# Gated attention and two MLP blocks on Trainium2: the input statistics taken as one maximum on VectorE, the gate's statistics on row sums of the output

## The chip, the core and the metric

The kernel runs on one core of a Trainium2 chip. The core has five engines with queues of their own, each working in order: TensorE (PE in the profile; its weight loads are PEld), VectorE (DVE), ScalarE (ACT), GpSimd (POOL) and SyncE (SP), which here issues all DMAs. They meet at semaphores: an instruction that reads what another engine or a DMA writes waits for it, and so does one that overwrites what another still reads. The metric is device time in microseconds; before the change its median is 695.99 us over three runs (694.93 to 697.37).

## The reference

Inputs q, k, v, alpha have 4 batches, 8 heads, 768 positions and head width 48. A gated linear attention is followed by a ReLU block and a gated block, both with residuals, all in float32:

```python
state = zeros(B, H, D, D)
for t in range(S):
    state = alpha[:, :, t, :, None] * state + einsum('bhd,bhe->bhde', k[:, :, t], v[:, :, t])
    y[:, :, t] = einsum('bhd,bhde->bhe', q[:, :, t], state)
x = y.transpose(0, 2, 1, 3).reshape(B, S, 384)
x = x + maximum(layer_norm(x) * g1 @ w1, 0) @ w2              # 384 -> 1536 -> 384
u, v = split(gelu_tanh(x @ w_in), 2)                          # 384 -> 1024
v = layer_norm(v) * g2
x = x + (u * (w_sg @ v + b_sg)) @ w_out                       # w_sg is 768 x 768 over positions
```

## The kernel before

The positions of a batch are cut into six chunks of 128 rows, so there are 24 chunks, and two neighbouring chunks form a group for the ReLU block. `split_path` computes everything with float32 numbers split into a high and a low float16 half, three matmul passes for each product. This is exact enough only while numbers stay in certain bounds, so it gathers statistics as it goes (`st_in` of the inputs, `st_fe` of the decay, `st_xs` and `st_xm` of the residual stream, `st_g` of the gate, `st_ws` of the weights). At its end a list `checks` compares them with bounds (three small DVE instructions for each entry, L1039 to L1041), the results are reduced to one flag `bad`, and only if it is set does `general_path` compute all of it again without splitting.

The work comes in steps and units. A chunk's attention is a list of steps (`att_steps`); the dense blocks are units: A (L675, matmuls into `pg`, then the two halves of `hT`, L680 on ACT and L681 on DVE), B (L709, L712), T (L730, transposes), C (L749, L774), D (the gate over positions: matmuls L794, `tm` on DVE L800, product on POOL L803, halves on ACT L804 and POOL L805, and a square with a sum on ACT, L807) and E (output matmuls L822, the residual added by DVE L824, the store L826). Steps and units have due times from a table of numbers, and Python emits them in that order; a scheduler of the tile framework then reorders instructions within each engine by a simulated timeline. What stands in an engine's queue is therefore read from the built program.

`load_chunk` (L236) loads alpha, q, k and v of a chunk into one of two buffers `inp`, so chunk i + 2 overwrites chunk i, operand by operand, as soon as the last reader of that operand is done. Readers are: for alpha, q and k the copies to `stage` on ACT (L295), whose tiles SP transposes by DMA (L298) and ACT copies once more (L311) before the decay scans on DVE (L351, L354); for v the split into two halves `vs` (L151 on ACT, L152 on DVE); and `stats` for all four. `stats` takes three squares with row sums on ACT (L532, for q, k and v) and one maximum of magnitudes on DVE (L534, for alpha). The first batch's six chunks, called whole, take no statistics, so `stats` runs for 18 chunks. The load of chunk i + 2 stands in the emitted order behind the `stats` of chunk i.

Of the kernel before, what the change touches and what calls it, by code (L numbers as in the profile page):

```python
# [7 lines left out]
F32 = mybir.dt.float32  # L8
# [4 lines left out]
AF = mybir.ActivationFunctionType  # L13
ALU = mybir.AluOpType
AX = mybir.AxisListType
PSUM = bass.MemoryType.PSUM

P = 128
# [35 lines left out]
def split_path(ctx, tc, ident, bad, q, k, v, alpha, g1, w1, w2, w_in, g2, w_sg, b_sg, w_out, out):  # L54


    nc = tc.nc
    B, H, S, D = q.shape
    DM = H * D
    NP = H // 2  # L60
    NCH = S // P
# [6 lines left out]
    NC = B * NCH  # L68
# [8 lines left out]
    big = ctx.enter_context(tc.tile_pool(name="big", bufs=1))  # L77
# [19 lines left out]
    st_in = big.tile([P, NC, 4], F32, name="st_in")  # L97
# [1 line left out]
    st_mv = big.tile([P, NC, 2], F32, name="st_mv")  # L99
    st_xs = big.tile([P, NC], F32, name="st_xs")  # L100
    st_xm = big.tile([P, NC], F32, name="st_xm")
    st_g = big.tile([P, NC], F32, name="st_g")
    st_ws = big.tile([P, 8 + NG3 + 2 * KD], F32, name="st_ws")
    st_w, st_wg, st_w1, st_wr = (st_ws[:, a:b] for a, b in ((0, 8), (8, 8 + NG3), (8 + NG3, 8 + NG3 + KD),
                                                            (8 + NG3 + KD, 8 + NG3 + 2 * KD)))
# [5 lines left out]
    def junk():  # L111
        return p2.tile([P, 512], BF16, tag="cv", name="junk")
# [141 lines left out]
    def att_steps(i, group, slot):  # L254
        b, c = divmod(i, NCH)
        t = inp[i % NIN]
# [133 lines left out]
        if i >= KA:  # L390
            n = NP * (P + 1)
# [124 lines left out]
        if whole:  # L516
            T["vs"] = t[:, 2, :, 0:D]
        else:
            @step
            def _():  # L520
                T["vs"] = p1.tile([P, 2, H, D], F16, tag="vs", name="vs")
                split2(T["vs"][:, 0], T["vs"][:, 1], t[:, 2, :, 0:D], S_V)

            stats_step[i] = len(steps)

            @step
            def _():
                stats()

        def stats():  # L530
            for n in range(3):
                nc.scalar.activation(out=junk()[:, 0:DM].rearrange("p (h d) -> p h d", h=H), in_=t[:, n, :, 0:D],  # L532
                                     func=AF.Square, accum_out=st_in[:, i, n:n + 1])
            nc.vector.tensor_reduce(out=st_in[:, i, 3:4], in_=t[:, 3, :, 0:D], op=ALU.max, axis=AX.XY,  # L534
                                    apply_absolute_value=True)

        @step
        def _():
# [120 lines left out]
    def A_units(j):  # L659


        units = []
        N, per = (P, KD) if j == 0 else (U, 512 // U)
        for part in range(U // N):
            for u in range(KF // per):
                def unit(u=u, part=part):
                    m = part if j == 0 else u // (KF // per // 2)
                    if (j, m) not in hT:
                        hT[j, m] = ring.tile([P, 2, KF * P], F16, tag="hT", bufs=2, name="hT")
                    pg = ps.tile([P, per, N], F32, tag="g", bufs=3, name="pg")  # L670
                    o = slice(part * N, (part + 1) * N)
                    for f in range(per):
                        ff = u * per + f
                        for n_, (kk, a, r) in enumerate([(kk, a, r) for kk in range(KD) for a, r in passes]):
                            nc.tensor.matmul(out=pg[:, f, :], lhsT=w1s[:, a, kk, ff * P:(ff + 1) * P],  # L675
                                             rhs=xhT[j][:, r, kk, o], start=(n_ == 0), stop=(n_ == 3 * KD - 1))
                    u0 = u if j == 0 else u % (KF // per // 2)
                    hi, lo = (hT[j, m][:, a, u0 * per * N:(u0 + 1) * per * N] for a in range(2))
                    src = pg.rearrange("p f t -> p (f t)")
                    nc.scalar.activation(out=hi, in_=src, func=AF.Relu)  # L680
                    last_dve[0] = nc.vector.scalar_tensor_tensor(out=lo, in0=src, scalar=0.0, in1=hi, op0=ALU.max,  # L681
                                                                 op1=ALU.subtract)
                units.append((unit, per * 9 * N / 2400.0, (2, 3, 5, 6)[((u + 1) * per - 1) // KD],
                              groups[j][0] * NCH + groups[j][1] + (part if j == 0 else 1)))
        return units
# [96 lines left out]
    def D_units(b):  # L782
        units = []
        for th in range(S // U):
            for dp in range(KG // 2):
                def unit(th=th, dp=dp):
                    key = (b, th)

                    gt[key] = uf[key].bitcast(F16).rearrange("p (g a f t) -> p g a f t", g=KG // 2, a=2, f=2)
                    pg = ps.tile([P, 2, U], F32, tag="g", bufs=3, name="pgs")  # L790
                    for f in range(2):
                        d = 2 * dp + f
                        for n_, (s, a, r) in enumerate([(s, a, r) for s in range(NCH) for a, r in passes]):
                            nc.tensor.matmul(out=pg[:, f, :], lhsT=vn[b * NCH + s][:, a, d * P:(d + 1) * P],  # L794
                                             rhs=wgs[th][:, r, s, :], start=(n_ == 0),
                                             stop=(n_ == 3 * NCH - 1))
                    tm = p2.tile([P, 2, U], F32, tag="tm", name="tm")
                    for f in range(2):
                        d = 2 * dp + f
                        nc.vector.scalar_tensor_tensor(out=tm[:, f, :], in0=pg[:, f, :], scalar=g2c[:, d:d + 1],  # L800
                                                       in1=bbc[:, th * U:(th + 1) * U], op0=ALU.mult, op1=ALU.add)
                    o = slice(2 * dp, 2 * dp + 2)
                    nc.gpsimd.tensor_tensor(out=tm, in0=tm, in1=uT[key][:, o, :], op=ALU.mult)  # L803
                    nc.scalar.activation(out=gt[key][:, dp, 0], in_=tm, func=AF.Copy)  # L804
                    nc.gpsimd.tensor_tensor(out=gt[key][:, dp, 1], in0=tm, in1=gt[key][:, dp, 0], op=ALU.subtract)  # L805
                    n_ = b * 6 + 2 * th + dp
                    nc.scalar.activation(out=junk()[:, 0:512].rearrange("p (a b) -> p a b", a=2), in_=tm,  # L807
                                         func=AF.Square, accum_out=st_g[:, n_:n_ + 1])
                units.append((unit, 36 * U / 2400.0, NW[3]))
        return units  # L810

    def E_units(b):
        units = []
        for c in range(NCH):
            def unit(c=c):
                i = b * NCH + c
                key = (b, c // 2)
                o = slice((c % 2) * P, (c % 2) * P + P)
                pg = ps.tile([P, DM], F32, tag="g", bufs=3, name="pgo")
                for d in range(KG):  # L820
                    for a, r in passes:
                        nc.tensor.matmul(out=pg, lhsT=gt[key][:, d // 2, a, d % 2, o], rhs=wos[:, r, d, :],  # L822
                                         start=(d == 0 and a == 0 and r == 0), stop=(d == KG - 1 and r == 1))
                nc.vector.scalar_tensor_tensor(out=xs[i], in0=pg, scalar=1.0 / (S_G * S_WO), in1=xs[i],  # L824
                                               op0=ALU.mult, op1=ALU.add)
                nc.sync.dma_start(out=out[b, c * P:(c + 1) * P, :], in_=xs[i])  # L826
            units.append((unit, 12 * DM / 2400.0, NW[4]))
        return units
# [30 lines left out]
    if True:  # L859
# [18 lines left out]
        for _ in range(2):  # L878
            t = ring.tile([P, KG * U], I32, tag="uT", bufs=3, name="bits")[:, 0:768]
# [13 lines left out]
        for kk in range(KD):  # L893
            nc.vector.tensor_scalar(out=diags[0][:, kk], in0=ident, scalar1=g1c[:, kk:kk + 1], scalar2=None,
                                    op0=ALU.mult)
# [40 lines left out]
        for j in range(NG + 1):  # L936
            starts.append(sum(x[1] for x in flat))
            seq = []
            if j < NG:
                a = A_units(j)  # L940
# [22 lines left out]
        def at(t):  # L963
            return D0 + min(t, DX) * DS + max(t - DX, 0.0)
# [9 lines left out]
        for j in range(NG):  # L974
            b, c, n = groups[j]
# [3 lines left out]
            for s in range(n):  # L979
                i = b * NCH + c + s  # L980
# [20 lines left out]
        for f, cost, need, *chunk in flat:  # L1001
            t = max([t, at(now)] + [emitted[i][-1] + 1e-3 for i in chunk])
# [6 lines left out]
        for _, kind, f, need in sorted(events, key=lambda x: x[:2]):  # L1009
# [8 lines left out]
        row_scale_window()  # L1018

        checks = [  # L1020
            (st_in[:, :, 0:3], 2.0 ** -2, 2.0 ** 12, [NC, 3]),
            (st_in[:, :, 3:4], 0.0, 1.0, [NC, 1]),
            (st_fe, 2.0 ** -100, 1.0, [NC, NP]),
            (st_xs, -1e30, 1e30, [NC]),
            (st_mv[:, :, 1:2], 2.0 ** -22 * S_Y ** 2, 2.0 ** 3 * S_Y ** 2, [NC, 1]),
            (st_xm, 2.0 ** -12, 2.0 ** 14, [NC]),
            (st_g, 0.0, 2.0 ** 31, [NC]),
            (st_w, 2.0 ** -2, 127.0, [8]),
            (st_wg, 2.0 ** -2, 6e4, [NG3]),
            (st_w1, 2.0 ** -2, 2000.0, [KD]),  # L1030
# [4 lines left out]
        for n, (src, lo, hi, shape) in enumerate(checks):  # L1035
# [6 lines left out]
                                    axis=AX.XY if len(shape) == 2 else AX.X)  # L1042
# [242 lines left out]
```

## Time and profile before

| | before |
|---|---|
| median of three runs | 695.99 us (694.93 to 697.37) |
| the profiled execution | 693.09 us, its span 691.3 us |
| mean granted TensorE clock | 0.982 |
| VectorE, 0 to 130 us | 113.70 us busy |
| TensorE, 0 to 130 us | 104.89 us busy, clock 0.95 |
| `L807` accumulator reads on ACT | 24 of 188 ns |
| squares of `x` on ACT, L732 (they stay) | 24 of 512 ns |

The profile was taken on one execution; the span runs from its first to its last instruction. A busy time is the time in which an engine had an instruction under way, an idle time is put down to what ended it. The rows that matter most stand beside the sentences that use them in the prediction.

### The profile page before, as it was taken

The page shows a single profiled execution, that of the slowest core. Times are in us where ns is not written, and L with a number is a line of the kernel's source. Part 1 is how long each engine was busy: PE and PEld are TensorE (multiplying, and loading weights), DVE is VectorE, ACT ScalarE, POOL GpSimd, SP SyncE. Part 2 cuts the span into 40 slices and gives each one's busy share as a digit, 9 for nine tenths or more (in the row PEclk, how much of TensorE's full clock was granted, in tenths as well). Part 3 has the DMA queues.
Part 4 walks back from the last instruction along what each step waited for, and adds up shares of the span by engine and source line. Part 5 has one row for each costly group of instructions (what it writes and reads, how often), then busy time and mean ns, then how long its engine had stood idle before and what let it go on. Part 6 is the DMA issues. An engine that isn't in the chain of part 4 may idle for free.

```text
span 691.3 us, 14364 instructions
## 1 busy us (share of the span) xinstructions
PE 639.3 (92%) x5622; PEld 485.9 (70%) x5622; DVE 445.4 (64%) x876; ACT 412.9 (60%) x787; POOL 242.7 (35%) x462
## 2 busy tenths in 40 slices
PE   5999579899999989999999988999999979999996
PEld 3787467677677876677777875676677867676783
DVE  7899868677744676557744678668666386333325
ACT  3765535667874589588765599767653764332230
POOL 2122011334423760433532860532405670302261
PEclk9999879999999998999999999999999999999999
DMA  9996797739482359366362169644251602200102
GB/s 227 279 233 193 206 236 157 133 64 131 68 120 43 51 101 164 99 119 108 70 109 46 39 109 206 123 70 73 50 81 29 103 17 64 29 13 12 35 2 73
DMA packets 228636, 70.63 MB, mean 102 GB/s; under 512 B 219472, under 2 KB 222544, under 8 KB 228560
## 3 DMA queue, kind: packets, MB, share of 16 engines
q1 hardware_dynamic: 228560, 69.63, 52.6%
q8 instruction: 46, 0.75, 0.5%
q14 instruction: 30, 0.25, 0.1%
HBM read 35.79 MB, written 4.72 MB: 59 GB/s over the span
## 4 chain that ended last, share of the span: by engine, by line
PE 43%; DVE 19%; ACT 13%; DMA 13%; POOL 5%; issue 3%; SPq 2%; ACTq 0%; DVEq 0%
PE pg L709 12%; PE pg L675 8%; PE pgo L822 6%; PE pgu L774 5%; DMA stage<-stage 5%; PE pgv L749 4%; PE pgs L794 3%; ACT stage L311 2%; DMA wgs<-wsp 2%; ACT stage L295 2%; DVE K L354 2%; ACT junk L532 2%; DVE F L354 2%; DMA inp<-in_q_dram 2%; DMA inp<-in_alpha_dram 2%
## 5 line engine op out<-in xcount | busy, mean ns | idle before, releaser
L675 PE MATMUL pg<-xhT,w1s 128*128 128x256 f16 (+1 forms) x1404 | 153.8, 269 | 8.0 <-DVE hT L681 7.4
L675 PEld LDWEIGHTS <-w1s 128*128 128x128 f16 x1404 | 130.1, 100 | 26.3 <-issue 8.2
L709 PE MATMUL pg<-w2s,hT 128*128 128x384 f16 x864 | 144.6, 326 | 0.3 <-DVE hT L681 0.3
L709 PEld LDWEIGHTS <-hT 128*128 128x128 f16 x864 | 83.7, 98 | 54.0 <-issue 0.5
L794 PE MATMUL pgs<-wgs,vn 128*128 128x256 f16 x864 | 96.0, 273 | 0.0
L794 PEld LDWEIGHTS <-vn 128*128 128x128 f16 x864 | 84.0, 98 | 10.4
L681 DVE SCALAR_TENSOR_TENSOR hT<-pg,hT 128x512 f16<-128x512 f32 (+1 forms) x74 | 49.5, 672 | 54.1 <-ACT hT L680 54.0
L311 ACT ACTIVATE stage<-stage 128x1024 uint16<-128x1024 uint16 x48 | 64.6, 1353 | 19.1 <-DMA stage<-stage 18.6
L295 ACT ACTIVATE stage<-inp 128x1024 uint16<-128x1024 uint16 x48 | 49.8, 1050 | 24.5 <-DVE K L354 12.6
L774 PE MATMUL pgu<-x2T,wis 128*128 128x256 f16 x432 | 50.1, 273 | 2.1 <-DVE hT L681 1.9
L822 PE MATMUL pgo<-wos,uT 128*128 128x384 f16 x288 | 48.6, 326 | 2.7 <-DVE hT L681 2.7
L680 ACT ACTIVATE hT<-pg 128x512 f16<-128x512 f32 (+1 forms) x74 | 42.1, 572 | 13.2 <-PE pg L675 13.1
L749 PE MATMUL pgv<-wis,x2T 128*128 128x512 f16 x216 | 49.4, 379 | 0.4 <-DVE x L824 0.3
L155 POOL TENSOR_TENSOR qs<-F,qs 128x512 f16<-128x512 f32 x18 | 20.5, 1138 | 80.2 <-ACT qs L422 80.1
L774 PEld LDWEIGHTS <-wis 128*128 128x128 f16 x432 | 41.6, 98 | 8.6 <-DVE hT L681 2.3
L155 POOL TENSOR_TENSOR kh<-K,kh 128x512 f16<-128x512 f32 x17 | 20.5, 1207 | 72.5 <-ACT kh L444 71.2
L822 PEld LDWEIGHTS <-uT 128*128 128x128 f16 x288 | 27.8, 98 | 21.1 <-issue 3.5
L800 DVE SCALAR_TENSOR_TENSOR tm<-pgs,g2c,bbc 128x256 f32<-128x256 f32 x48 | 20.9, 476 | 32.6 <-PE pgs L794 14.8
L803 POOL TENSOR_TENSOR tm<-tm,uT 128x512 f32<-128x512 f32 x24 | 33.3, 1387 | 15.5 <-DVE tm L800 15.5
L749 PEld LDWEIGHTS <-x2T 128*128 128x128 f16 x216 | 20.7, 98 | 22.6 <-issue 0.6
L804 ACT ACTIVATE uT<-tm 128x512 f16<-128x512 f32 x24 | 14.9, 622 | 34.2 <-POOL tm L803 34.2
L805 POOL TENSOR_TENSOR uT<-tm,uT 128x512 f16<-128x512 f32 x24 | 28.2, 1174 | 17.2 <-ACT uT L804 17.2
(175 smaller groups left out, 1094.2 us busy)
## 6 DMA issues: line engine op xcount, KB each, us to landing
stage<-in_moe_w_ch_dram SPq DMA_DIRECT2D x24, 384.0 KB, 5.0
inp<-in_alpha_dram SPq DMA_DIRECT2D x24, 192.0 KB, 3.4
inp<-in_q_dram SPq DMA_DIRECT2D x24, 192.0 KB, 3.6
inp<-in_k_dram SPq DMA_DIRECT2D x24, 192.0 KB, 4.0
inp<-in_v_dram SPq DMA_DIRECT2D x24, 192.0 KB, 4.0
out_dram<-x SPq DMA_DIRECT2D x24, 192.0 KB, 2.1
stage<-in_moe_w_in_dram SPq DMA_DIRECT2D x4, 768.0 KB, 4.6
stage<-in_moe_w_sg_dram SPq DMA_DIRECT2D x6, 384.0 KB, 3.7
```

Source lines behind the costliest of these rows:

```text
L155: (nc.vector if on_dve else nc.gpsimd).tensor_tensor(out=out, in0=in0, in1=in1, op=ALU.subtract)
L295: nc.scalar.activation(out=sp, in_=t[:, n].rearrange("p h d -> p (h d)").bitcast(U16) .rearrange("p (x w) -> p w x", w=2), func=AF.Copy)
L311: nc.scalar.activation(out=words[:, :, :, gap:], in_=tr, func=AF.Copy)
L675: nc.tensor.matmul(out=pg[:, f, :], lhsT=w1s[:, a, kk, ff * P:(ff + 1) * P], rhs=xhT[j][:, r, kk, o], start=(n_ == 0), stop=(n_ == 3 * KD ...
L680: nc.scalar.activation(out=hi, in_=src, func=AF.Relu)
L681: last_dve[0] = nc.vector.scalar_tensor_tensor(out=lo, in0=src, scalar=0.0, in1=hi, op0=ALU.max, op1=ALU.subtract)
L709: nc.tensor.matmul(out=box[s], lhsT=hidden(a, f, s), rhs=w2s[:, r, f, :], start=(f == 0 and a == 0 and r == 0), stop=(f == KF - 1 and r == 1))
L749: nc.tensor.matmul(out=pg, lhsT=x2T[j][:, a, kk, o], rhs=wis[:, r, kk, DG:DI], start=(n_ == 0), stop=(n_ == 3 * KD - 1))
L774: nc.tensor.matmul(out=pg[:, f, :], lhsT=wis[:, a, kk, ff * P:(ff + 1) * P], rhs=x2T[j][:, r, kk, 0:N], start=(n_ == 0), stop=(n_ == 3 * K ...
L794: nc.tensor.matmul(out=pg[:, f, :], lhsT=vn[b * NCH + s][:, a, d * P:(d + 1) * P], rhs=wgs[th][:, r, s, :], start=(n_ == 0), stop=(n_ == 3 ...
L803: nc.gpsimd.tensor_tensor(out=tm, in0=tm, in1=uT[key][:, o, :], op=ALU.mult)
L822: nc.tensor.matmul(out=pg, lhsT=gt[key][:, d // 2, a, d % 2, o], rhs=wos[:, r, d, :], start=(d == 0 and a == 0 and r == 0), stop=(d == KG ...
```

## The change

`stats` becomes one instruction on DVE: the largest magnitude of each row of q, k, v and alpha in one reduction of 128x1536 to 128x4. The bounds on q, k and v become bounds on a magnitude rather than on a sum of squares. The gate's square on ACT (L807) is kept for the last batch alone; for the other three batches the output's residual addition on DVE also leaves its row sum in a new tile `st_o`, which one more entry of `checks` compares with ±1e30.

```diff
-    st_g = big.tile([P, NC], F32, name="st_g")
+    st_g = big.tile([P, 6], F32, name="st_g")
+    st_o = big.tile([P, NC - NCH], F32, name="st_o")
...
         def stats():
-            for n in range(3):
-                nc.scalar.activation(out=junk()[:, 0:DM].rearrange("p (h d) -> p h d", h=H), in_=t[:, n, :, 0:D],
-                                     func=AF.Square, accum_out=st_in[:, i, n:n + 1])
-            nc.vector.tensor_reduce(out=st_in[:, i, 3:4], in_=t[:, 3, :, 0:D], op=ALU.max, axis=AX.XY,
-                                    apply_absolute_value=True)
+            nc.vector.tensor_reduce(out=st_in[:, i, :], in_=t[:, :, :, 0:D], op=ALU.max, axis=AX.XY, apply_absolute_value=True)
...
-                    n_ = b * 6 + 2 * th + dp
-                    nc.scalar.activation(out=junk()[:, 0:512].rearrange("p (a b) -> p a b", a=2), in_=tm,
-                                         func=AF.Square, accum_out=st_g[:, n_:n_ + 1])
+                    if b == B - 1:
+                        n_ = 2 * th + dp
+                        nc.scalar.activation(out=junk()[:, 0:512].rearrange("p (a b) -> p a b", a=2), in_=tm,
+                                             func=AF.Square, accum_out=st_g[:, n_:n_ + 1])
...
                 nc.vector.scalar_tensor_tensor(out=xs[i], in0=pg, scalar=1.0 / (S_G * S_WO), in1=xs[i],
-                                               op0=ALU.mult, op1=ALU.add)
+                                               op0=ALU.mult, op1=ALU.add,
+                                               accum_out=st_o[:, i:i + 1] if b < B - 1 else None)
...
-            (st_in[:, :, 0:3], 2.0 ** -2, 2.0 ** 12, [NC, 3]),
+            (st_in[:, :, 0:3], 2.0 ** -3, 3.25, [NC, 3]),
...
-            (st_g, 0.0, 2.0 ** 31, [NC]),
+            (st_g, 0.0, 2.0 ** 31, [6]),
+            (st_o, -1e30, 1e30, [NC - NCH]),
```

The lines move: the maximum is L532 in the changed kernel, and lines between there and L800 have a number smaller by three (hT's DVE half is L678, the `vs` and `xsp` splits are L153). Since every load now hangs on another instruction, the scheduler's order changes in more places than the diff touches.

The first place is DVE between chunks 11 and 13, near 246 to 257 us of the profile before. The two `inp` buffers are inp_94 and inp_95 before, inp_95 and inp_96 after, for even and odd chunks. Before:

```order
L155 TENSOR_TENSOR ss_3034<-sc,ss_3034 128x512
L800 SCALAR_TENSOR_TENSOR tm<-pgs,g2c,bbc 128x256 x2
L534 TENSOR_REDUCE st_in<-inp_94 128x1
L800 SCALAR_TENSOR_TENSOR tm<-pgs,g2c,bbc 128x256 x2
L609 TENSOR_TENSOR state<-psd,state 64x4x48 x2
L621 BN_STATS bs<-psy 128x6
L623 BN_AGGR st_mv<-bs 128x2
L625 TENSOR_SCALAR nmu<-st_mv 128x1
L152 SCALAR_TENSOR_TENSOR vs<-inp_95,vs 128x384
L628 SCALAR_TENSOR_TENSOR xsp<-psy,st_mv,xsp 128x384
L152 SCALAR_TENSOR_TENSOR xsp<-x,xsp 128x384
L681 SCALAR_TENSOR_TENSOR hT<-pg,hT 128x512
```

After, at the same place of the program:

```order
L797 SCALAR_TENSOR_TENSOR tm<-pgs,g2c,bbc 128x256 x4
L606 TENSOR_TENSOR state<-psd,state 64x4x48 x2
L618 BN_STATS bs<-psy 128x6
L620 BN_AGGR st_mv<-bs 128x2
L622 TENSOR_SCALAR nmu<-st_mv 128x1
L153 SCALAR_TENSOR_TENSOR vs<-inp_96,vs 128x384
L625 SCALAR_TENSOR_TENSOR xsp<-psy,st_mv,xsp 128x384
L153 SCALAR_TENSOR_TENSOR xsp<-x,xsp 128x384
L678 SCALAR_TENSOR_TENSOR hT<-pg,hT 128x512 x2
L532 TENSOR_REDUCE st_in<-inp_96 128x4
L678 SCALAR_TENSOR_TENSOR hT<-pg,hT 128x512
L480 TENSOR_TENSOR sc<-sc,causal 128x512
```

The alpha maximum between the `tm` pairs is gone. The maximum of all four operands of chunk 13 stands four instructions behind the `vs` of chunk 11, the last reader of the v that the load of chunk 13 overwrites, and between two halves of `hT`.

The second place is SP's queue for the loads of chunks 12 to 14, at about the same time. Before:

```order
L236 DMA inp_94<-in_alpha_dram 128x8x48
L451 DMA_TRANSPOSE ks<-kh 128x8x128
L236 DMA inp_94<-in_q_dram 128x8x48
L236 DMA inp_94<-in_k_dram 128x8x48
L236 DMA inp_94<-in_v_dram 128x8x48
L642 DMA_TRANSPOSE xhT<-xsp 128x6x128
L730 DMA_TRANSPOSE x2T<-xsp 128x6x128
L298 DMA_TRANSPOSE stage<-stage 128x8x128 x2
L236 DMA inp_95<-in_q_dram 128x8x48
L236 DMA inp_95<-in_k_dram 128x8x48
L730 DMA_TRANSPOSE x2T<-xsp 128x6x128
L236 DMA inp_95<-in_v_dram 128x8x48
```

After (the first two rows load chunk 13, the third chunk 12's v):

```order
L237 DMA inp_96<-in_q_dram 128x8x48
L237 DMA inp_96<-in_k_dram 128x8x48
L237 DMA inp_95<-in_v_dram 128x8x48
L639 DMA_TRANSPOSE xhT<-xsp 128x6x128
L299 DMA_TRANSPOSE stage<-stage 128x8x128
L237 DMA inp_95<-in_alpha_dram 128x8x48
L299 DMA_TRANSPOSE stage<-stage 128x8x128 x2
L237 DMA inp_95<-in_q_dram 128x8x48
L452 DMA_TRANSPOSE ks<-kh 128x8x128
L237 DMA inp_95<-in_k_dram 128x8x48
L237 DMA inp_96<-in_v_dram 128x8x48
```

Before, q and k of chunk 12 are issued just ahead of their own transposes (the row with x2). After, q and k of chunk 13 and even of chunk 14 are issued about there, only v keeps its place behind `vs`, and the alpha load of chunk 14 stands ahead of the transposes of chunk 12's q and k.

The third place is DVE at the start, near 108 to 111 us, where chunk 6, the first that is not whole, begins. Before, from the page's timeline, no maximum stands there. After:

```order
L620 BN_AGGR st_mv<-bs 128x2
L384 RECIPROCAL rf<-rf 128x4
L532 TENSOR_REDUCE st_in<-inp_95 128x4
L622 TENSOR_SCALAR nmu<-st_mv 128x1
L352 SCALAR_TENSOR_TENSOR F<-pt,rf,consts 128x128 x4
```

The maximum of chunk 6 has come in almost directly ahead of the four scans (the profile names this row TENSOR_TENSOR_SCAN) of the last whole chunk. Its predecessor, the alpha maximum of chunk 6, stood at 82.53 us in the profile before.

## The prediction

> **What bounds the kernel now.** I read the page first, its busy times and its chain of work that ended last.
>
> ```profile
> span 691.3 us, 14364 instructions
> PE 639.3 (92%) x5622; PEld 485.9 (70%) x5622; DVE 445.4 (64%) x876; ACT 412.9 (60%) x787; POOL 242.7 (35%) x462
> PE 43%; DVE 19%; ACT 13%; DMA 13%; POOL 5%; issue 3%; SPq 2%; ACTq 0%; DVEq 0%
> ```
>
> TensorE is the bound: 639.3 of 691.3 us. The change takes no matmul away, so all that it can win lies in the 52.0 us in which PE stands still, and in stretches where its clock is low. ACT and DVE matter only where PE waits for them. Next came the busy time by stretch (columns: stretch, PE, weight loads, DVE, ACT, POOL, granted clock, DMA share, GB/s) and, for the middle of the run, the list of what PE waited for (us, times, longest).
>
> ```profile
> 130.00:250.00 120.00, 115.74 (x1097) 89.36 (x1096) 73.64 (x144) 81.87 (x157) 55.36 (x105) 1.00 0.55 85
> 250.00:270.00 20.00, 16.89 (x130) 12.71 (x129) 15.01 (x28) 20.00 (x47) 7.48 (x11) 0.83 0.75 143
> 270.00:402.00 132.00, 131.16 (x1217) 98.67 (x1215) 79.81 (x150) 89.89 (x168) 57.41 (x105) 1.00 0.49 88
> 402.00:424.00 22.00, 16.38 (x150) 13.09 (x148) 15.07 (x28) 21.79 (x49) 8.34 (x13) 1.00 0.84 144
> 424.00:600.00 176.00, 168.97 (x1518) 125.50 (x1516) 115.50 (x199) 107.52 (x213) 70.75 (x135) 0.99 0.41 73
> ...
> PE pg L675 <- DVE hT L681: 7.4, 5, 2.7
> PE psy L588 <- ACT ss L498: 2.9, 2, 1.5
> PE pgo L822 <- DVE hT L681: 2.7, 4, 2.2
> ```
>
> Two short stretches stand out, 250 to 270 and 402 to 424: ACT is full (20.00 of 20, 21.79 of 22) and PE idles 3.1 and 5.6 us. In the first the clock is 0.83 besides; 16.89 us of PE work at 0.83 would take 14.0 at 1.00, so some 2.9 us more are lost. PE's other idle time between 130 and 600 is 4.3 + 0.8 + 7.0 = 12.1 us. The chain within 246 to 270 says what ACT is full of (by line, then a piece of it: start, us, what); behind it stands PE's longest gap in each stretch.
>
> ```profile
> by line: ACT junk L532 17.4%; DMA stage<-stage 13.2%; ACT stage L311 13.0%; ACT hT L680 10.4%; ACT stage L295 8.7%; issue 5.8%; ACT junk L807 5.1%; ACT junk L732 4.2%; ACT uT L804 4.1%; ACT ss L498 4.0%; ACT xsp L151 3.4%; DVE hT L681 2.9%;
> 251.35 0.50 ACT junk L532 x2
> ...
> 257.98 4.00 PE L675 MATMUL pg<-xhT,w1s 128*128 128x256 f16 x18 [2.75 <-DVE hT L681]
> 411.75 2.12 PE L675 MATMUL pg<-xhT,w1s 128*128 128x256 f16 x18 [2.60 <-DVE hT L681]
> ```
>
> Statistics squares (L532, L807) hold 22.5% of that chain, 5.4 of 24 us, and the ReLU halves hT, for which PE waits in both gaps, queue behind them.
>
> **The change part by part.** The groups with the durations (columns: busy us, mean ns of one | idle before, cause):
>
> ```profile
> L532 ACT ACTIVATE junk<-inp 128x384 bf16<-128x384 f32 x54 | 27.6, 512 | 1.1 <-DVE mvv L756 1.1
> L532 ACT ACTIVATION_READ_ACCUMULATOR junk<-inp 128x1 f32 x54 | 10.3, 191 | 0.0
> L807 ACT ACTIVATE junk<-tm 128x512 bf16<-128x512 f32 x24 | 14.7, 614 | 0.0
> L534 DVE TENSOR_REDUCE st_in<-inp 128x1 f32<-128x384 f32 x18 | 9.9, 549 | 25.4 <-DMA inp<-in_alpha_dram 25.3
> L835 DVE TENSOR_REDUCE st_ws<-w1s 128x1 f32<-128x1536 f16 x3 | 5.1, 1743 | 0.0
> L824 DVE SCALAR_TENSOR_TENSOR x<-pgo,x 128x384 f32<-128x384 f32 x24 | 13.1, 550 | 6.8 <-PE pgo L822 6.6
> L712 DVE SCALAR_TENSOR_TENSOR x<-pg,rx,x 128x384 f32<-128x384 f32 x24 | 14.7, 613 | 21.3 <-PE pg L709 21.2
> L712 DVE DVE_READ_ACCUMULATOR x<-pg,rx,x 128x1 f32 x24 | 2.0, 83 | 0.0
> ```
>
> *Squares on ACT.* All 54 of L532 go, and 18 of the 24 of L807 (all but the last batch's). Asked for these lines alone, the stretches answer (us, ACT busy and count; the first two rows are L532, the third L807):
>
> ```profile
> 248.00:270.00 22.00, 4.79 (x16) 0.84 0.78 146
> 402.00:424.00 22.00, 4.82 (x16) 1.00 0.84 144
> ...
> 248.00:270.00 22.00, 1.41 (x4) 0.84 0.78 146
> ```
>
> That is eight squares of L532 with their accumulator reads and two of L807 in each: 6.2 us busy. The next instruction starts some 0.1 us before such a pair ends (0.50 from start to start in the piece at 251.35), so 6.2 − 10 × 0.1 = 5.2 us of ACT time come free in each, 10.4 together, against 3.1 + 2.9 + 5.6 = 11.6 lost there. So the gain lies between 0 and −10.4. What is late next are the transposes of the staged operands and the ACT copies L311 and L295 around them, 34.9% of the same chain, with DMA at 0.75 and 0.84 of its time. I take two thirds, **−7**.
>
> On the clock: behind the gap of 2.75 us 18 matmuls take 4.00 us, behind that of 2.60 the same 18 take 2.12. The Trainium skill, TensorE: Matmul & The Clock Gate, Part 1: The HAM clock gate, has the clock halve after an idle window of about 3.4 us that runs freely. By that page gaps of this length need not cost clock; were the 2.9 us owed to something else, two thirds of them, 1.9, would fall out of the gain. The trace shows the dip at 2.75 us, so I keep them.
>
> *Loads that waited for squares.* A load of q, k or v overwrites what the square of two chunks earlier read, so SP, which issues in order, waits for ACT:
>
> ```profile
> SPq L236 <- ACT junk L532: 22.6, 22, 4.2
> 503.25 1.06 ACT L295 ACTIVATE stage<-inp 128x1024 uint16<-128x1024 uint16 x1 [2.35 <-DMA inp<-in_q_dram]
> 500.69 4.09 PE L675 MATMUL pg<-xhT,w1s 128*128 128x256 f16 x36 [0.72 <-DVE hT L681]
> 505.57 1.69 PE L675 MATMUL pg<-xhT,w1s 128*128 128x256 f16 x14 [0.79 <-DVE hT L681]
> inp<-in_v_dram SPq DMA_DIRECT2D x24, 192.0 KB, 4.0
> ```
>
> At 503 ACT waited 2.35 us for such a q, and PE lost 0.72 + 0.79 about it. In the new order q and k stand about a chunk earlier on SP, but each load, alpha too, now waits for the DVE maximum of the chunk two before. I take −1 here and −2 for the rest of the 12.1 us, since ACT loses 54 × 0.51 + 18 × 0.61 = 38.5 of its 412.9 us but PE's other waits come from many links; bounds 0 and −12.1: **−3**.
>
> *The maximum on DVE.* A reduce of 128x1536 took 1.743 us (L835, f16 in; the nearest row), one of 128x384 0.549; four of these would be 2.2. I take 1.74. So 18 × (1.743 − 0.549) = 21.5 us more DVE work. The row sums on the output add, by L712 beside L824, 18 × (0.613 − 0.550 + 0.083) = 2.6. DVE goes to some 470 of 690 us, most of it under PE's work.
>
> The wait matters more. Before, the reduce stalled DVE for alpha, 25.3 us in 13 places. Now it needs v as well, and v can only be loaded when `vs` of the chunk two before has read the old one. In the rows at chunk 13 four instructions like L712's 0.61 (two xsp, two hT) stand between, 2.4 us, and v takes 4.0 to land: a stall of 1.6; elsewhere one such and small ones stand between, a stall near 2.6. Twelve of them come to 19 to 31 us: the stalls are swapped, not added. What is new is that 1.74 + 1.6 = 3.3 us of blocked DVE stand in front of an hT, in five places by the order. PE has three buffers for these groups and fills one in half of the 4.09 us above, 2.0; with two filled ahead and 1.2 us for the two halves of one hT (ACT and DVE), cover is about 2.9 us. So 0.4 × 5 = **+2**. Bounds: 0 (all under PE), and 24.1 (all added work on the path).
>
> Such a stall already cost something, the alpha wait ahead of this hT:
>
> ```profile
> 475.19 0.55 DVE L534 TENSOR_REDUCE st_in<-inp 128x1 f32<-128x384 f32 x1 [2.79 <-DMA inp<-in_alpha_dram]
> 476.66 0.68 DVE L681 SCALAR_TENSOR_TENSOR hT<-pg,hT 128x512 f16<-128x512 f32 x1
> ```
>
> *Start-up.* The first two alpha maxima leave the loading phase. The new one of chunk 6 stands right ahead of the scans at 110.49, for which PE waits, and those of chunks 7 and 8 before kh and vg, just behind the reduce at 132.94.
>
> ```profile
> 110.49 1.60 DVE L351 TENSOR_TENSOR_SCAN F<-pt,rf,consts 128x128 f32<-128x128 f32 x4
> 132.94 0.55 DVE L534 TENSOR_REDUCE st_in<-inp 128x1 f32<-128x384 f32 x1 [3.19 <-DMA inp<-in_alpha_dram]
> ```
>
> At worst both 1.74 land on PE (+3.5), at best two short reduces less are gained (−0.5; they stood beside other loads). I take the middle, **+1.5**.
>
> *Tail.* One more check is three more small DVE instructions. They stand ahead of the verdict, and the last output tile follows it:
>
> ```profile
> 684.26 0.14 DVE L1046 CAST bad<-verdict 1x1 int32<-1x1 f32 x1 [1.51 <-POOL verdict L1045]
> 685.27 0.56 DVE L824 SCALAR_TENSOR_TENSOR x<-pgo,x 128x384 f32<-128x384 f32 x1 [0.40 <-PE pgo L822]
> ```
>
> Three instructions of the size of this CAST, 0.14, delay the CAST by 0.3 to 0.5; 0.40 us of idling ahead of the last tile cover most: **+0.1**, bounds 0 and +0.5.
>
> **Sum:** −7 − 3 + 2 + 1.5 + 0.1 = −6.4, span 684.9. The profiled execution took 693.09, 1.8 above its span, so it becomes 686.7. The median shown is 695.99, 2.9 above that execution; on that scale the forecast is **689.6**.
>
> **Rivals.**
>
> *Slower: the wait for v lands on the path.* Place: the reduces between 130 and 600. Price: the blocked stretch grows from 0.55 + 25.3/13 = 2.5 us to 1.74 + 1.9 = 3.6, 1.1 more, 13 times: +14.3. It decides if the cover ahead of those places is nearer 2.5 than 2.9 us, so that every added microsecond shows, hT, scans and, through the next alpha load on SP, the transposes queued behind it included. With −10 from ACT and +3.5 at the start the sum is +8: 704. For: PE waits for hT in two of the rows above, 10.1 us; DVE is at 15 of 20 and 15 of 22 in the full stretches. Against: in 270 to 402 PE idles 0.8 of 132 us though alpha stalls were there too. The Trainium skill, VectorE: DVE Perf Modes, Rules for kernel authors, calls tensor_reduce on a hot path the slowest DVE operation and advises restructuring; 1743 ns for 1536 elements agrees, and the rule speaks for this rival.
>
> *No change.* The transposes and their copies are late right behind ACT, so the full stretches give only −3 and the rest −1; DVE +2 and start-up +1.5 stay: −0.4, 695.6. For: DMA at 0.75 to 0.84 there. Against: q and k come earlier.
>
> *A larger gain.* Both full stretches clear (−10.4), half the 12.1 goes (−6), DVE costs 1 and the start nothing: −15.4, 680.6. Against: DVE gets no lighter.
>
> *The change doesn't do what it says:* a check that fails on the new bounds (2⁻³ to 3.25) would add the general path, far above any time here. The inputs q, k, v have width 0.1, and the largest of 384 lies near 0.3; chance under 0.01.
>
> **How the numbers follow.** Some 0.3% of the time, 2.1 us, is what a measurement can tell from no change: faster is below 693.9, slower above 698.1. The forecast's own case, 683.5 to 693.9, has 0.49; the larger gain 0.15; no change 0.19; slower 0.17. So faster 0.64, same 0.19, slower 0.17. Half of the slower case and most of the larger gain belong in the range: 680 to 700.
>
> **What would show it.** Right: no ACT junk but L732 in the full stretches, ACT below 90% and PE idle there cut by about two thirds; a reduce near 1.74 us that waits for v, some 19 to 31 us in all; DVE near 470 us. Wrong: PE's waits for hT grow with the reduce right ahead of hT in DVE's timeline (the slower rival); or the same PE gaps with the transposes in place of the squares (no change); or a reduce far from 1.74 us.

## The result and the profile after

The changed kernel is slower: 705.85 us median (704.33 to 709.99, four runs) against 695.46 for the kernel before on the same chip, a ratio of 1.017 with a 95% interval of 1.014 to 1.020. The forecast was 689.6, with a range of 680 to 700. The page of the changed kernel, the same lines as before:

```profile
span 704.4 us, 14233 instructions
PE 641.4 (91%) x5622; PEld 486.8 (69%) x5622; DVE 461.4 (66%) x897; ACT 375.7 (53%) x643; POOL 240.9 (34%) x462
PE 46%; DVE 21%; DMA 13%; ACT 10%; issue 6%; POOL 2%; SPq 2%; ACTq 0%; DVEq 0%; POOLq 0%
```

The work moved nearly as costed: ACT lost 37.2 us of busy time (38.5 costed), PE has the same 5622 matmuls, and DVE gained 16.0 (24.1 costed). The maximum and the row sums cost DVE about what was forecast; its other work is shorter in the new order (without any statistics, below, DVE is busy for 432.5 us in the new order and 439.4 in the old). But PE now stands still for 63.0 us instead of 52.0, and the chain of work that ended last names ACT less and DVE more. Busy time by stretch (the columns as before), and what PE waited for behind the start-up:

```profile
130.00:250.00 120.00, 110.42 (x983) 82.71 (x981) 74.95 (x140) 70.88 (x125) 48.37 (x100) 0.97 0.56 89
250.00:270.00 20.00, 15.12 (x177) 13.34 (x175) 10.77 (x20) 13.95 (x23) 14.27 (x14) 0.95 0.55 84
270.00:402.00 132.00, 123.89 (x1085) 90.05 (x1084) 81.49 (x154) 81.68 (x138) 42.99 (x94) 0.98 0.53 95
...
PE pg L672 <- DVE hT L678: 12.6, 6, 3.1
PE psd L549 <- ACT vs L152: 4.2, 2, 3.6
PE sc L467 <- ACT K L459: 2.7, 1, 2.7
```

ACT is no longer full between 250 and 270 (13.95 of 20, before 20.00), and yet PE idles 4.9 us there and not 3.1. From 130 to 250 its idle time grows from 4.3 to 9.6 us, from 270 to 402 from 0.8 to 8.1, and the clock, 1.00 before in both stretches, is 0.97 and 0.98. Since the changed kernel is behind by then, the work of the two full stretches lies later in it, near 258 to 280 and 418 to 440:

```profile
258.00:280.00 22.00, 15.40 (x133) 12.63 (x132) 14.51 (x25) 15.17 (x26) 9.92 (x14) 0.84 0.69 112
418.00:440.00 22.00, 18.21 (x193) 15.32 (x192) 15.57 (x27) 15.98 (x27) 9.94 (x14) 0.92 0.66 111
```

ACT is busy for 15.17 and 15.98 of 22 us, and PE idles 6.6 and 3.8 us. The forecast's sign of being right, PE's idle time there cut by about two thirds, did not come. PE waits for hT more than before, and for `vs` and K on ACT, an engine with idle time. The groups that the change touched:

```profile
L532 DVE TENSOR_REDUCE st_in<-inp 128x4 f32<-128x1536 f32 x18 | 31.5, 1750 | 18.7 <-DMA inp<-in_v_dram 14.2 <-issue 4.1 <-DMA inp<-in_k_dram 0.4
...
L822 DVE SCALAR_TENSOR_TENSOR x<-pgo,x 128x384 f32<-128x384 f32 x24 | 13.1, 553 | 8.8 <-PE pgo L820 8.7
...
L822 DVE DVE_READ_ACCUMULATOR x<-pgo,x 128x1 f32 x18 | 1.5, 83 | 0.0
```

The maximum takes 1.750 us, and DVE stands idle for 18.7 us in front of it in all: 14.6 us are put down to the loads of v and k, for 4.1 the profile shows no cause (`issue`). The row sums cost 1.5 us and nothing in the instruction itself (553 ns, before 550).

### The profile page after: what moved, and what is told of

It reads as the page before. It is cut to its first block, busy times and chain, and to the rows that moved or that the text cites. A ratio compares the mean times of both kernels' runs of the same rounds, so it can differ in the third digit from the quotient of the medians.

```text
span 704.4 us, 14233 instructions
## 1 busy us (share of the span) xinstructions
PE 641.4 (91%) x5622; PEld 486.8 (69%) x5622; DVE 461.4 (66%) x897; ACT 375.7 (53%) x643; POOL 240.9 (34%) x462
## 4 chain that ended last, share of the span: by engine, by line
PE 46%; DVE 21%; DMA 13%; ACT 10%; issue 6%; POOL 2%; SPq 2%; ACTq 0%; DVEq 0%; POOLq 0%
PE pgs L791 12%; PE pg L706 10%; PE pg L672 7%; DMA stage<-stage 6%; PE pgv L746 4%; PE pgu L771 3%; PE pgo L820 3%; ACT stage L312 2%; DVE hT L678 2%; DMA inp<-in_v_dram 2%; ACT stage L296 2%; DVE F L355 2%; DVE K L355 2%; PE sc L467 1%; DVE sc L480 1%
## 5 line engine op out<-in xcount | busy, mean ns | idle before, releaser
L672 PE MATMUL pg<-xhT,w1s 128*128 128x256 f16 (+1 forms) x1404 | 154.2, 271 | 15.0 <-DVE hT L678 12.6
L791 PEld LDWEIGHTS <-vn 128*128 128x128 f16 x864 | 84.0, 98 | 10.4
L678 DVE SCALAR_TENSOR_TENSOR hT<-pg,hT 128x512 f16<-128x512 f32 (+1 forms) x74 | 48.7, 670 | 25.7 <-ACT hT L677 25.5
L532 DVE TENSOR_REDUCE st_in<-inp 128x4 f32<-128x1536 f32 x18 | 31.5, 1750 | 18.7 <-DMA inp<-in_v_dram 14.2
L800 POOL TENSOR_TENSOR tm<-tm,uT 128x512 f32<-128x512 f32 x24 | 32.6, 1361 | 10.2 <-DVE tm L797 10.2
```

## The experiments

Two theories. **Order**: the time follows from where the scheduler put everything else (copies, transposes, loads) once the loads hung on another instruction. **DVE**: the maximum and its wait for v hold DVE ahead of hT and the scans. To part them, the emitted instructions of an engine were held in a recorded order, that of the kernel before ("old") or of the changed kernel ("new"), by edges that fix the order of issue and add no wait. Statistics were then put in or left out; where squares were put into the new order and the maximum into the old one, the scheduler chose the places of the statistics themselves. The function that holds the order, shortened:

```diff
+def pin_order(tc, stats, engines=("PE", "DVE", "Activation", "Pool", "SP")):
...
+        for a, b in zip(seq, seq[1:]):
+            tc.add_manual_dep(by[e][b], by[e][a].name,
+                              mybir.DependencyInfo(mybir.DependencyClass.NoSync, mybir.DependencyReason.DATA),
+                              reason="order")
```

**Squares in the new order** (the squares write a tile of their own, so that they can stand anywhere):

```diff
-                nc.scalar.activation(out=junk()[:, 0:DM].rearrange("p (h d) -> p h d", h=H), in_=t[:, n, :, 0:D],
+                nc.scalar.activation(out=jq.rearrange("p (h d) -> p h d", h=H), in_=t[:, n, :, 0:D],
```

> The statistics of before (three squares on ACT, alpha maximum on DVE, gate squares), with every other instruction of each engine held in the order that it has in the changed kernel; the squares write a scratch tile of their own. Theory 'order' (the time follows from where the staging copies, transposes and loads now stand, not from the maximum): as slow as the changed kernel or slower, 704 to 712. Theory 'wait for v' (the maximum's 1.75 us and its wait block DVE ahead of hT and the scans): no maximum, so near the kernel before, 694 to 699.

709.27 us, ratio 1.019 (1.015 to 1.023). No maximum of four operands is in it (only alpha's short one), and it is no faster than the changed kernel (1.017).

**No statistics**, in either order: `stats` returns at once, the gate's square and `accum_out` go, `st_in`, `st_g` and `st_o` are set to one.

> No input statistics, no gate squares and no row sums at all (their checks read ones), the rest in the order of before. Both theories: the squares cost something in the full stretches, so faster than before, 685 to 692. If it is above 694, the squares on ACT were never worth anything.

> No input statistics, no gate squares, no row sums (their checks read ones), the rest in the order of the changed kernel. 'Order': still slow, 698 to 704. 'Wait for v': the block on DVE is gone, so 685 to 692, like the same work in the old order.

682.48 us, ratio 0.983 (0.979 to 0.987), in the old order; 693.06, ratio 0.998 (0.995 to 1.001), in the new. The same work, 10.6 us apart by order alone, less than the order theory said and more than the other. All statistics of the kernel before together, the squares, the alpha maxima with their waits and all 24 gate squares, are worth 694.36 − 682.48 = 11.9 us in the old order; no run parts the squares from the alpha maxima.

**Maximum in the old order**, with alpha apart, since the old order loads alpha ahead of the other three:

```diff
-            nc.vector.tensor_reduce(out=st_in[:, i, :], in_=t[:, :, :, 0:D], op=ALU.max, axis=AX.XY, apply_absolute_value=True)
+            nc.vector.tensor_reduce(out=st_in[:, i, 3:4], in_=t[:, 3, :, 0:D], ...)
+            nc.vector.tensor_reduce(out=st_in[:, i, 0:3], in_=t[:, 0:3, :, 0:D], ...)
```

> The statistics of the changed kernel, but the maximum in two pieces (alpha alone, then q, k and v in one instruction of 128x1152), the rest in the order of before. 'Order': 686 to 694. 'Wait for v': the long piece still waits for v on DVE, so 700 to 706.

700.51 us, ratio 1.008 (1.006 to 1.011): 18.0 above no statistics in that order, more than the 11.9 of the old statistics. So DVE costs too. Both theories hold a part; the next four kernels take the DVE part to pieces, with every instruction, the maxima too, in its place in the changed kernel.

**Time without wait, wait without time, no row sums:**

```diff
-            nc.vector.tensor_reduce(out=st_in[:, i, :], in_=t[:, :, :, 0:D], op=ALU.max, axis=AX.XY, ...)
+            nc.vector.tensor_reduce(out=st_in[:, i, :], in_=w1s[:, 0, 0].rearrange("p (a b) -> p a b", a=4), ...)   # first
+            nc.vector.tensor_reduce(out=st_in[:, i, :], in_=t[:, :, 0:1, 0:8], op=ALU.max, axis=AX.XY, ...)         # second
...
-                                               accum_out=st_o[:, i:i + 1] if b < B - 1 else None)                      # third
```

> Every instruction of the changed kernel in its own place, but the 18 maxima read a resident weight tile of the same 1536 elements instead of the inputs (their bounds are opened): the DVE time stays, the wait for v and the hold on the next loads go. No statistics in this order took 693.1, the changed kernel 705.9. Theory 'DVE time': 703 to 706. Theory 'wait for v': 695 to 698. Both in parts: 698 to 703.

> Every instruction in its own place, but the 18 maxima read 8 columns of one head of each operand, 32 elements instead of 1536 (bounds opened): the waits for all four loads and the hold on the next loads stay, the DVE time goes, about 18 x 1.6 = 29 us of busy time. 'DVE time': 693 to 697. 'Wait for v': 702 to 706.

> The changed kernel in its own order without the row sums of the output (no check of batches 0 to 2): 2.6 us of DVE work less, all of it beside PE. Both theories: 704.5 to 706.

698.95 us (ratio 1.006, 1.004 to 1.008), 695.36 (1.002, 1.000 to 1.004) and 705.79 (1.018, 1.013 to 1.023). Above the 693.06 without statistics, DVE time alone costs 5.9 us, the waits alone 2.3, both together 12.8; the row sums cost nothing that these runs can tell. The 2.3 can hardly be told from nothing either, for the runs without statistics lie between 689.65 and 698.12. The two parts don't add up, and one place shows why. From the changed kernel, two rows of DVE and one of PE (start, length, idle before):

```profile
324.07 1.75 DVE L532 TENSOR_REDUCE st_in<-inp 128x4 f32<-128x1536 f32 x1 [2.57 <-issue]
325.74 0.68 DVE L678 SCALAR_TENSOR_TENSOR hT<-pg,hT 128x512 f16<-128x512 f32 x1
...
326.47 3.76 PE L672 MATMUL pg<-xhT,w1s 128*128 128x256 f16 x33 [1.70 <-DVE hT L678]
```

The same place with a few columns:

```profile
316.09 0.19 DVE L555 TENSOR_REDUCE st_in<-inp 128x4 f32<-128x32 f32 x1 [2.45 <-issue]
316.19 0.68 DVE L701 SCALAR_TENSOR_TENSOR hT<-pg,hT 128x512 f16<-128x512 f32 x1
...
316.92 3.33 PE L695 MATMUL pg<-xhT,w1s 128*128 128x256 f16 x29
```

And with resident data:

```profile
317.02 1.75 DVE L555 TENSOR_REDUCE st_in<-w1s 128x4 f32<-128x1536 f16 x1
318.68 0.68 DVE L702 SCALAR_TENSOR_TENSOR hT<-pg,hT 128x512 f16<-128x512 f32 x1
...
320.30 1.92 PE L696 MATMUL pg<-xhT,w1s 128*128 128x256 f16 x16
```

A block of 2.45 + 0.19 = 2.6 us in front of hT costs PE nothing, and one of 1.75 nothing; 2.57 + 1.75 = 4.3 costs 1.70. The cover, the time that PE can go on without this hT, is about 2.6 us here, and only the two together go beyond it. The profile puts the 2.45 and 2.57 us to `issue`, so it names no cause for them; with resident data there is no idle time in front of any of the 18 maxima, so they hang on the inputs.

Set side by side, PE's waits in the four profiles show where the rest lies (us; one profile each, all in the new order):

| PE waits for | none | a few columns | resident data | changed |
|---|---|---|---|---|
| the scans (F), near 112 to 115 us | 0.18 | 1.06 | 1.26 | 3.11 |
| K on ACT, near 156 to 161 | 0.30 | 0.92 | 3.02 | 2.74 |
| `vs` on ACT, near 258 to 268 | 2.07 | 2.59 | 1.87 | 3.61 |
| hT, near 326 and 364 in the changed kernel | 0 | 0 | 0.34 | 1.70 + 1.46 |
| hT, near 193 to 199 | 3.06 | 3.09 | 3.09 | 3.07 |
| hT, near 506 to 521 | 2.67 | 2.68 | 2.68 | 2.68 |
| PE idle in the whole span | 52.1 | 52.3 | 54.3 | 63.0 |
| PE busy (a lower clock makes it longer) | 638.3 | 641.2 | 644.3 | 641.4 |

At the scans, too, each part alone costs about 1 us and both cost 3. The two long waits for hT near 199 and 521 are there without any maximum: they belong to the order. With resident data most of what is lost is longer PE busy time, at a mean granted clock of 0.972 against 0.982 without statistics, not idle time.

**The order taken to pieces.** In the new order without statistics, ACT and then PE, near 251 to 261 us (start, length, idle before; L340 is the copy of a transposed operand):

```profile
251.60 1.26 ACT L487 ACTIVATE K<-K,rf 128x128 f32<-128x128 f32 x4
252.76 0.62 ACT L829 ACTIVATE uT<-tm 128x512 f16<-128x512 f32 x1
254.29 1.36 ACT L340 ACTIVATE stage<-stage 128x1024 uint16<-128x1024 uint16 x1 [0.91 <-DMA stage<-stage]
255.51 0.61 ACT L451 ACTIVATE qs<-F 128x512 f16<-128x512 f32 x1
256.02 1.35 ACT L340 ACTIVATE stage<-stage 128x1024 uint16<-128x1024 uint16 x1
257.22 0.52 ACT L639 ACTIVATE sp<-state 128x384 f16<-128x384 f32 x1
257.62 0.53 ACT L175 ACTIVATE vs<-inp 128x384 f16<-128x384 f32 x1
...
258.20 0.24 PE L577 MATMUL psd<-vs,ks 128*128 128x96 f16 x2 [2.07 <-ACT vs L175]
259.19 0.29 PE L577 MATMUL psd<-vs,ks 128*128 128x96 f16 x3 [0.75 <-DVE vs L176]
261.36 2.93 PE L700 MATMUL pg<-xhT,w1s 128*128 128x256 f16 x13 [1.88 <-DVE hT L706]
```

q and k of the next chunk are loaded earlier in this order, and the copies of their transposes stand ahead of `sp`, `vs`, xsp and hT in ACT's queue (that the scheduler put them there because of the earlier loads is read from the two orders; its own timeline was not looked at). ACT waits for the DMA transpose (0.91 us) and then copies for 2.5 us, with the dense path behind it; PE loses 2.07 + 0.75 + 1.88 us. The changed kernel itself has the same queue, and PE loses 3.61 + 0.68 + 1.77 us behind it:

```profile
261.27 1.25 ACT L459 ACTIVATE K<-K,rf 128x128 f32<-128x128 f32 x4
264.13 1.34 ACT L312 ACTIVATE stage<-stage 128x1024 uint16<-128x1024 uint16 x1 [1.09 <-DMA stage<-stage]
265.85 1.33 ACT L312 ACTIVATE stage<-stage 128x1024 uint16<-128x1024 uint16 x1
267.45 0.51 ACT L152 ACTIVATE vs<-inp 128x384 f16<-128x384 f32 x1
...
268.01 0.32 PE L549 MATMUL psd<-vs,ks 128*128 128x96 f16 x2 [3.61 <-ACT vs L152]
```

The test moves 23 such copies back past at most six instructions of the dense path (the expectations say five), in the recorded order of ACT and nowhere else:

```python
for i in reversed(range(len(rows))):            # ACT's order: rank and source line of each instruction
    if rows[i][1] == COPY:                      # stage<-stage
        j = i
        while j + 1 < len(rows) and j - i < 6 and rows[j + 1][1] in DENSE:   # sp, vs, xsp, hT, x's square, uT, qs
            j += 1
        rows.insert(j, rows.pop(i))
```

> No input statistics, no gate squares, no row sums, the order of the changed kernel, except on ACT: 23 copies of transposed operands (stage from stage) are moved back past up to five instructions of the dense path that stood right behind them (vs, sp, xsp, hT, the squares of x, uT, qs). The same work took 693.1 in the new order and 682.5 in the old. Theory 'copies wait for transposes ahead of the dense path': 683 to 688. If the order costs elsewhere: 692 to 695, or worse because the copies now come late for the scans.

> The changed kernel, each instruction in its own place but for the same 23 copies. Changed kernel 705.9. Theory 'copies ahead of the dense path' with a separate DVE cost of some 13: 695 to 700. If the maximum on DVE holds the path by itself: 703 to 707.

678.96 us (ratio 0.977, 0.973 to 0.980) and 689.51 (0.992, 0.989 to 0.995): 14.1 and 16.4 us less than in the new order as the scheduler left it. The same place, now:

```profile
249.85 1.27 ACT L487 ACTIVATE K<-K,rf 128x128 f32<-128x128 f32 x4
251.01 0.63 ACT L829 ACTIVATE uT<-tm 128x512 f16<-128x512 f32 x1
251.53 0.63 ACT L451 ACTIVATE qs<-F 128x512 f16<-128x512 f32 x1
252.05 0.53 ACT L639 ACTIVATE sp<-state 128x384 f16<-128x384 f32 x1
252.46 0.53 ACT L175 ACTIVATE vs<-inp 128x384 f16<-128x384 f32 x1
...
258.46 0.58 PE L577 MATMUL psd<-vs,ks 128*128 128x96 f16 x5 [2.19 <-DMA ks<-kh]
258.85 3.38 PE L700 MATMUL pg<-xhT,w1s 128*128 128x256 f16 x17
```

`vs` starts 2.6 us behind K's start and not 6.0; what PE waits for is now the next link, the transpose of kh, and hT is not waited for.

**Mixed orders**, no statistics: SP's order new and the rest old, then PE's, DVE's and POOL's new and ACT's and SP's old.

> No statistics; SP (all loads, transposes, stores) in the order of the changed kernel, the four other engines in the order of before. 682.5 with all five as before. If earlier loads of q and k hurt by themselves (transposes queued behind loads): 687 to 693. If it is ACT's order that hurts: 681 to 685.

> No statistics; PE, DVE and POOL in the order of the changed kernel, ACT and SP in that of before. If ACT's order makes the 10.6: 681 to 686. If PE's or DVE's order makes it: 690 to 695.

701.29 us (ratio 1.010, 1.007 to 1.013) and 697.71 (1.004, 1.002 to 1.006), both slower than either whole order (682.5, 693.1). They don't tell which engine's order is at fault: queues that were ordered to fit one another make new waits when half of them is exchanged. In the first, PE waits 17.3 us in three places for the transpose of kh (ks), 1.2 us with all queues in the new order.

**Controls**: whether moving the copies helps the old order as much, 26 of them there.

> Control: no statistics, the order of before, with the copies of transposed operands moved back by the same rule (26 of them here). In this order it took 682.5. If the copies ahead of the dense path are the new order's own fault: 680 to 684, little gain. If the rule helps any order as much: 668 to 675.

> Control: the kernel before, all its statistics, each instruction in its own place but for the same 26 copies. If the new order's own fault: 691 to 697. If the rule helps any order as much: 680 to 686, and then the changed kernel with copies later (689.5) is still the slower of the two.

678.90 us (0.977, 0.974 to 0.980) and 692.00 (0.996, 0.994 to 0.998): 3.6 and 2.7 us less. In the new order the same rule was worth 14.1 and 16.4. Without statistics the two orders now take the same time, 678.9 and 679.0, so the places of these copies account for the 10.6 us between them, within the spread of the runs.

**The gate part alone**, first as the scheduler orders it, then with 21 copies moved back:

> The gate part of the change alone (squares of the gate for the last batch only, row sums of the output), the input statistics as before; the scheduler orders it. 18 pairs of 0.61 us leave ACT, 2.6 us come to DVE. If the order stays close to before: 690 to 694. If every edit reshuffles the order by as much as this one did: anywhere from 690 to 706.

> The gate part of the change alone (688.95 in its own order), with 21 copies moved back by the same rule. If the rule helps where copies stand ahead of the dense path: 680 to 687, the fastest complete kernel here. If not: 687 to 690.

688.95 us (0.991, 0.988 to 0.993) and 683.79 (0.984, 0.981 to 0.986). Both are complete kernels and faster than the kernel before and the changed one. The first has an order of its own, so its gain is the gate part and that order together. All medians, in us (the kernel before took 694.1 to 695.5 beside these sets):

| statistics | old order | new order | old, copies later | new, copies later |
|---|---|---|---|---|
| none | 682.5 | 693.1 | 678.9 | 679.0 |
| squares on ACT (before) | 694.4 | 709.3 | 692.0 | not run |
| maximum on DVE | 700.5 (alpha apart) | 705.9 (changed) | not run | 689.5 |
| squares, gate part changed | 689.0 (its own order) | | 683.8 (its own order) | |

The rows for squares and maximum tell what made the change slow. In the changed kernel's order the old statistics are no faster than the new ones (709.3 and 705.9), and with the copies moved back they aren't either (692.0 and 689.5). Only in the old order are the new ones dearer, by 6.1 us (700.5 for 694.4, with alpha apart). So the changed kernel is slow by the order that came with the exchange, and not because the new statistics would cost more than the old ones in that order. The changed kernel with its copies later is a complete kernel and faster than the kernel before (689.51 against 695.05 beside it). That this is the forecast's 689.6 is luck: the new statistics cost 689.51 − 678.96 = 10.5 us even there, three times the 3.5 that were forecast for the maximum and the start-up.

## Why the prediction was wrong

By the table the change is: old statistics away −11.9, new order +10.6, maximum in (with the six gate squares and row sums that stay) +12.8, together +11.5; measured +10.4, the rest being the 1 us by which the sets differ. The parts depend on the order in which they are taken: with the old statistics in, the new order costs 709.27 − 694.36 = 14.9.

- *Squares on ACT and loads that waited for them*, −7 and −3: about right, as far as it is shown. The −11.9 in the old order takes in the alpha maxima and the six gate squares that stay, so it is not the squares' alone. The profile without statistics in the old order has, in the places of the two full stretches:

```profile
250.00:270.00 20.00, 17.24 (x147) 12.79 (x146) 15.34 (x23) 17.82 (x32) 10.18 (x13) 1.00 1.17 161
400.00:424.00 24.00, 20.85 (x190) 15.31 (x188) 20.51 (x28) 20.64 (x34) 9.75 (x13) 1.00 1.08 183
```

The clock of 0.83 is back at 1.00, worth the 2.9 us of the prediction, and PE idles 2.8 and 3.2 us in place of 3.1 and 5.6. That is some 5.7 us, near the −7, but little of it in the first stretch is idle time.

- *The step that failed is the one on the loads.* It counted q and k a chunk earlier on SP as a gain, and the rival of no change named it as evidence against itself ("q and k come earlier"). I compared SP's and DVE's rows of the two orders and not ACT's. In the new order the copies of q and k stand further up in ACT's queue, ahead of `vs`, xsp and hT, and there they wait for transposes: +10.6 (14.9 with the old statistics in), which is not in the sum at all. The sentence that the transposes and copies are late next in the full stretches named the right instructions and gave them only a share of the gain.
- *The maximum on DVE*, +2, and the *start-up*, +1.5: right in mechanism, far too small, 12.8 in place of 3.5. The duration was right (1.750 for 1.743), the cover nearly (2.6 seen at 324 us, 2.9 worked out), and the stalls in all were even a little shorter than forecast (18.7 us for 19 to 31). Too small was the block where it counts: 1.6 us of wait were taken, 2.57 were seen at 324 us. But hT in front of PE is only 3.2 us of it (1.70 + 1.46). More came at the start: against no statistics in the same order PE waits 2.9 us more for the scans at 115 us and 2.4 more for K at 161, 5.4 in all, beyond the bound of 3.5; a further 1.5 came at `vs` near 268. And an excess over the cover was priced as itself, while the clock can be lower behind a gap (below).
- *Row sums and tail*, nothing and +0.1: right, as far as the runs can tell. 705.79 without row sums for 705.85 with them; in front of the last output tile DVE still idles for PE (0.50 us, before 0.40), and the tile ends 5.4 us ahead of the span's end, before 5.5.
- *The slower rival*, 704, gave almost the time, by luck. PE's waits for hT did grow (12.6 us in six places, 7.4 before), but four of the six (3.07, 1.77, 1.88, 2.68) are there without any maximum too (3.06, 1.88, 1.89, 2.67): the order made them. Only 1.70 and 1.46 come with the maximum. Its 14.3 us are close to the 12.8, which lie in large part elsewhere, and it reached 704 without the order's 10.6. The advice to keep tensor_reduce off a hot path (the Trainium skill, VectorE: DVE Perf Modes, Rules for kernel authors) fits the 5.9 us that DVE time alone cost. That it is the slowest DVE operation is not what this trace shows: in the kernel before the reduce of 128x384 takes 549 ns, the SCALAR_TENSOR_TENSOR rows of that shape 550 and 613, and the 1743 ns for 1536 elements that the prediction took as agreeing don't compare it with another operation.

What stays open: why the waits for K at 161 us and `vs` at 268 grew was not followed link by link, the mixed orders were not followed further, and the place of each part rests on one profile of each kernel.

## What to carry to other kernels

Where a change moves loads earlier under a scheduler that reorders, compare the order of every strict queue, those that do the follow-up work on the loaded data first: an instruction whose data is loaded earlier may now stand, and wait, ahead of the critical path. A wait and a duration in front of a critical instruction are priced together against the cover there, since each alone may be free. And split a change into its parts before judging it, the order that the scheduler makes of it among them: the gate part alone, in its own order, gained 0.9%; the maximum, with the order that came with it, lost that and more; with 23 copies moved back the whole change gained 0.8%.

## What the runs showed of the hardware that was not expected

PE's granted clock was low behind many gaps of well under 3 us, though not behind each. Ten of these profiles (before, changed, and eight of the experiments) hold 28 PE gaps longer than 2.0 us, up to 3.6, behind the loading phase. In the 4 us behind 19 of them the granted clock was between 0.50 and 0.78, behind nine it was 1.00. Length alone doesn't decide: a gap of 2.03 us was followed by 0.63, one of 3.11 by 1.00. Nor does a gap have to be that long when others are near: in the kernel before the clock was 0.57 from 564 to 568 us, behind gaps of 1.49, 0.70 and 1.62 us. Two stretches of 4 us behind the gap of 3.61 us at 268 in the changed kernel (columns as before):

```profile
268.01:272.01 4.00, 1.55 (x10) 1.01 (x10) 3.69 (x5) 2.80 (x6) 2.94 (x6) 0.50 0.54 96
272.01:276.01 4.00, 4.00 (x26) 3.06 (x25) 3.78 (x5) 1.31 (x3) 0.00 (x0) 0.67 0.27 52
```

At 0.50 and 0.67, the 1.55 and 4.00 us in which PE was busy lose 1.55 × 0.50 + 4.00 × 0.33 = 2.1 us against full clock, on top of the 3.61 us of the gap; the shorter gaps right behind it (0.68 and 1.77 us) may have their part in the 2.1. The Trainium skill, TensorE: Matmul & The Clock Gate, Part 1: The HAM clock gate, speaks of an idle window of about 3.4 us that runs freely; that the window runs freely fits the scatter, but of the 19 gaps with a low clock behind them, 18 were shorter than it.
